# Casting and turning x three slices sooner, ahead of the next load in the SyncE queue

## The chip, the cores and the metric

The kernel runs on one core of one Trainium2 chip. The metric is device time in microseconds, as the median of several executions. Every execution also reports its span on the core and the mean granted clock of TensorE. An execution is called slow here when it is over 1.5% above the fastest of the same kernel; comparisons use the fast ones.

## The reference

For each of 8 batches (8 heads, 512 tokens, 32 state rows, head size 64), tokens and state attend to each other, and all rows then go through a gated layer:

```python
scores  = scale * x @ state.T          # 512 x 32 per head; softmax; xread = a  @ state
scores2 = scale * state @ x.T          # 32 x 512 per head; softmax; sread = a2 @ x
h   = concat([xread, sread])           # 544 rows per batch, 512 wide, for 8 batches
out = (relu(h @ w_gate) * (h @ w_val)) @ w_out      # 512 -> 1536 -> 512
```

## The kernel before

All matmuls are in bf16. The first two batches and the start of the third are written out as a list of first steps. A repeated part then runs one period per batch `s`, in 12 slices `jf`. In period `s` TensorE computes the gated layer of batch `s`. In the gaps the kernel computes the scores of batch `s+1` and prepares x of batch `s+2`: x is cast to bf16 (`x_conv`), turned by a transposing DMA (`x_bar`) into the layout that the scores need, and copied beside columns of ones (`x_copy`) for the sread matmuls.

```python
def x_conv(b, h0, n, eng):      # b >= 2: xb (bf16) <- xf (fp32), half of the heads at a time
    ...
def x_bar(b):                   # "the turn": 16 blocks of 128 x 128, 512 KB in all
    nc.sync.dma_start_transpose(out=xT[b].rearrange("p c j t -> p (c j) t"), in_=xb[b])
def x_dma(b, ...):              # "the load": 1 MB of x into xf (two buffers)
    ...  nc.sync.dma_start(out=xf[b][:, lo:lo + n], in_=x_rows(b, lo, n))
...
def nxt(n, jf):                 # n = s + 2
    if n >= B:
        return
    if jf == 6:
        xb_alloc(n)
        at_alloc(n)
        x_conv(n, 0, 4, "p")    # "p": GpSimd
    elif jf == 7:
        x_conv(n, 4, 4, "p")
        if n + 1 < B:
            x_dma(n + 1)
    elif jf == 9:
        x_bar(n)
    elif jf in (10, 11):
        x_copy(n, 2 * (jf - 10), 2, "p")

for s in range(2, B):
    for jf in range(NF):
        gv(s, jf)
        if jf in (3, 9):
            continue
        outp()                  # a third of an output tile; each third one evicts and issues a store
        for k in ((jf - 1, jf) if jf in (4, 10) else (jf,)):
            aux(s + 1, k)       # jf 0, 1: scores; 2, 3: normalise; 4: turn of the weights (ans)
            nxt(s + 2, k)
        if jf in (2, 8):
            ...                 # projections of w by the state (u_mm), their evictions, sread at 8
```

Loads, turns and stores all go through the SyncE queue, which in the traces issues them in program order and waits at each for what that one needs: in before an output stood in the queue from 69.6 us until its eviction let it go at 73.41, and the turn behind it went out at 75.06. From 60 to 192 us the outputs waited 18 times for their evictions, 71.5 us in all.

The softmax here doesn't subtract the row's maximum and nothing guards it: scores larger than these inputs give would overflow.

Of the kernel before, what the change touches and what calls it, by code (L numbers as in the profile page):

```python
# [67 lines left out]
def kernel(  # L68
# [55 lines left out]
    def cp(eng, o, i):  # L124
        if eng == "a":
            nc.scalar.copy(out=o, in_=i)  # L126
        elif eng == "v":
            nc.vector.tensor_copy(out=o, in_=i)  # L128
        else:
            nc.gpsimd.tensor_copy(out=o, in_=i)  # L130
# [22 lines left out]
    def x_dma(b, lo=0, n=H, after=None):  # L153
        if b not in xf:
            xf[b] = xin.tile([128, H, NC, D], FP32, name="xf", tag="xf")
        d = nc.sync.dma_start(out=xf[b][:, lo:lo + n], in_=x_rows(b, lo, n))  # L156
        loads["x", b, lo] = d.ins.name
        gate(d, after)
# [48 lines left out]
    def xb_alloc(b):  # L207
        xb[b] = att.tile([128, NC * H * D], BF16, name="xb", tag="xb", bufs=2)

    def at_alloc(b):  # L210
        xT[b] = att.tile([128, NC, NJ, 128], BF16, name="xT", tag="xT")
        e_sn[b] = att.tile([128, NC, 2, NJ, Ns], BF16, name="e_sn", tag="e_sn")
        asn[b] = att.tile([128, NC, 2, NJ, Ns], BF16, name="a_sn", tag="a_sn")
        cs[b] = small.tile([128, NC, 2, NJ], FP32, name="cs", tag="cs")
        rc[b] = small.tile([128, NC, 2, NJ], FP32, name="rc", tag="rc")
        ANS[b] = anspool.tile([128, NC, 2, 128], BF16, name="ans", tag="ans")
# [8 lines left out]
    def xs_rows(b, h0, n):  # L225
        v = xs(b)[:, :, h0 // 2:(h0 + n) // 2, 2:130]
        return v.rearrange("p c j (s d) -> p j s c d", s=2)

    def x_conv(b, h0, n, eng):
        src = xf[b][:, h0:h0 + n]  # L230
        if b < 2:
            cp(eng, xs_rows(b, h0, n), src.rearrange("p (j s) c d -> p j s c d", s=2))
        else:
            cp(eng, xb[b].rearrange("p (c h d) -> p h c d", h=H, c=NC)[:, h0:h0 + n], src)

    def x_copy(b, c0, n, eng):
        cp(eng, xs(b)[:, c0:c0 + n, :, 2:130],
           xb[b].rearrange("p (c j m) -> p c j m", c=NC, j=NJ)[:, c0:c0 + n])
# [12 lines left out]
    def x_bar(b):  # L251
        nc.sync.dma_start_transpose(out=xT[b].rearrange("p c j t -> p (c j) t"), in_=xb[b])
# [257 lines left out]
    def nxt(n, jf):  # L510
        if n >= B:
            return
        if jf == 6:
            xb_alloc(n)
            at_alloc(n)
            x_conv(n, 0, 4, "p")
        elif jf == 7:
            x_conv(n, 4, 4, "p")
            if n + 1 < B:
                x_dma(n + 1)  # L520
        elif jf == 9:
            x_bar(n)
        elif jf in (10, 11):
            x_copy(n, 2 * (jf - 10), 2, "p")

# [6 lines that stand above are left out]
            outp()  # L532
            for k in ((jf - 1, jf) if jf in (4, 10) else (jf,)):
                aux(s + 1, k)
                nxt(s + 2, k)
            if jf in (2, 8):
                if s + 1 < B:
                    if jf == 2:
                        u_alloc(s + 1)
                    else:  # L540
                        sr_mm(s + 1)
                    u_mm(s + 1, 768 * (jf // 8), 768)
                    if jf == 8:
                        sr_ev(s + 1)
                    for i, e in enumerate("avavav"):
                        u_ev(s + 1, 768 * (jf // 8), 768, i, e)
                outp()
# [36 lines left out]
```

## Time and profile before

| | before |
|---|---|
| time, three runs that the prediction knew | 225.16 us (224.95 to 225.21) |
| span of the profiled run | 222.4 us |
| TensorE busy | 215.7 us, 97% |
| VectorE, ScalarE, GpSimd busy | 63%, 51%, 19% |
| one period of the repeated part | 23.3 us |

In the profile PE is TensorE's matmuls, PEld its weight loads, DVE VectorE, ACT ScalarE, POOL GpSimd, SPq the SyncE queue. `xT<-xb` is the turn of x, `xf<-in_x_dram` the load of x, `sc_ps` the scores, which are the first readers of the turned x.

### The profile page before, as it was taken

How to read it: one execution, taken by the hardware profiler on the slowest of the kernel's cores; microseconds unless marked ns; L12 is line 12 of the kernel's file. 1: busy time of each engine (PE TensorE's matmuls, PEld its weight loads, DVE VectorE, ACT ScalarE, POOL GpSimd, SP SyncE). 2: the span in 40 equal slices, each digit the busy share in tenths (PEclk: the TensorE clock that was granted, in tenths of full speed). 3: DMA queues.
4: the chain of work that ended last, by engine and by line, in shares of the span. 5: the costliest groups of instructions: out<-in, count | busy, mean ns of one | idle time of the engine just before them, and what ended most of it. 6: DMA issues, size and time to landing. Idle time of an engine off the chain costs nothing.

```text
span 222.4 us, 4870 instructions
## 1 busy us (share of the span) xinstructions
PE 215.7 (97%) x1953; PEld 105.2 (47%) x1953; DVE 141.1 (63%) x245; ACT 114.4 (51%) x212; POOL 41.8 (19%) x51
## 2 busy tenths in 40 slices
PE   6979999999999999999999999999999999999994
PEld 3544434444444444444444444444444444586543
DVE  5789798697395748764786659565956543452210
ACT  3768776655463647364636374545546343343111
POOL 6498005064070330016000700000000000000000
PEclk9999999999999999999999999999999999999999
DMA  6999998979936831576138811351131111111133
GB/s 187 246 225 200 220 246 149 236 215 144 283 104 146 249 86 47 107 234 142 48 73 264 134 48 36 101 123 50 47 94 58 47 47 50 47 47 41 57 77 112
DMA packets 43575, 28.17 MB, mean 127 GB/s; under 512 B 23840, under 2 KB 39328, under 8 KB 43552
## 3 DMA queue, kind: packets, MB, share of 16 engines
q1 hardware_dynamic: 36688, 23.14, 39.3%
q0 software_dynamic: 6864, 4.72, 14.2%
q8 instruction: 15, 0.25, 0.4%
q14 instruction: 8, 0.07, 0.1%
HBM read 18.35 MB, written 8.91 MB: 123 GB/s over the span
## 4 chain that ended last, share of the span: by engine, by line
PE 89%; DMA 7%; DVE 1%; SPq 1%; issue 0%; ACT 0%
PE o_ps L414 38%; PE gv_ps L377 37%; PE u_ps L325 6%; PE gvs_ps L399 5%; DMA xf<-in_x_dram 4%; DMA xT<-xb 2%; PE sc_ps L260 1%; PE o_ps L439 1%; PE sr_ps L306 1%; SPq L156 1%; PE aT_ps L288 1%; DVE xs L128 1%; DVE U L128 0%; DVE ans L128 0%; SPq L142 0%
## 5 line engine op out<-in xcount | busy, mean ns | idle before, releaser
L386 DVE TENSOR_TENSOR h_sb<-gv_ps,g_sb 128x512 bf16<-128x512 f32 x96 | 65.5, 688 | 49.2 <-ACT g_sb L383 48.9
L377 PE MATMUL gv_ps<-ans,U 128*128 128x512 bf16 x384 | 94.5, 379 | 0.0
L414 PE MATMUL o_ps<-wo_sb,h_sb 128*128 128x512 bf16 x372 | 94.1, 379 | 0.0
L383 ACT ACTIVATE g_sb<-gv_ps 128x512 bf16<-128x512 f32 x96 | 57.3, 597 | 54.5 <-PE gv_ps L377 53.9
L377 PEld LDWEIGHTS <-U 128*128 128x128 bf16 x384 | 36.0, 98 | 42.1 <-issue 1.4
L414 PEld LDWEIGHTS <-h_sb 128*128 128x128 bf16 x372 | 35.3, 98 | 43.3 <-issue 4.0
L126 ACT CAST U<-u_ps 128x512 bf16<-128x512 f32 x52 | 27.7, 595 | 5.8 <-PE u_ps L325 5.2
L128 DVE CAST U<-u_ps 128x512 bf16<-128x512 f32 x44 | 27.7, 674 | 0.8 <-PE u_ps L325 0.8
L130 POOL CAST xb<-xf 128x1024 bf16<-128x1024 f32 x11 | 11.2, 1040 | 71.3 <-DMA xf<-in_x_dram 71.3
L126 ACT COPY o_sb<-o_ps 128x512 f32<-128x512 f32 (+2 forms) x20 | 10.8, 540 | 18.7 <-PE o_ps L414 17.1
L128 DVE COPY o_sb<-o_ps 128x512 f32<-128x512 f32 (+2 forms) x18 | 11.5, 637 | 9.1 <-ACT o_sb L126 4.5
L271 ACT ACTIVATE e_sn<-sc_ps 128x512 bf16<-128x512 f32 (+1 forms) x18 | 9.8, 552 | 9.8 <-PE sc_ps L260 9.8
L130 POOL COPY xs<-xb 128x1024 bf16<-128x1024 bf16 x11 | 11.2, 1042 | 1.0 <-DVE xb L128 0.7
L403 DVE TENSOR_TENSOR hs_sb<-gvs_ps,g_sb 128x256 bf16<-128x256 f32 x12 | 5.1, 425 | 9.8 <-ACT g_sb L402 9.8
L277 DVE TENSOR_REDUCE cs<-e_sn 128x32 f32<-128x1024 bf16 (+2 forms) x13 | 10.4, 801 | 0.4 <-ACT e_sn L271 0.2
L325 PE MATMUL u_ps<-wg_sb,stT 64*32 64x256 bf16 (+1 forms) x280 | 10.2, 315 | 0.0
L325 PEld LDWEIGHTS <-stT 64*32 64x32 bf16 x560 | 6.0, 90 | 8.5 <-issue 6.9
L402 ACT ACTIVATE g_sb<-gvs_ps 128x256 bf16<-128x256 f32 x12 | 4.6, 384 | 10.2 <-PE gvs_ps L399 7.8
L325 PE MATMUL u_ps<-wv_sb,stT 64*32 64x256 bf16 (+1 forms) x280 | 9.7, 309 | 0.0
L468 PE MATMUL warm_ps<-warm 128*128 128x256 bf16 x37 | 7.0, 314 | 1.1 <-DVE warm L470 1.1
L260 PEld LDWEIGHTS <-xT 128*128 128x128 bf16 x128 | 5.9, 98 | 4.3 <-DMA xT<-xb 0.9
L260 PE MATMUL sc_ps<-stT,xT 128*128 128x64 bf16 x128 | 7.0, 193 | 0.5 <-ACT xT L126 0.3
(52 smaller groups left out, 110.2 us busy)
## 6 DMA issues: line engine op xcount, KB each, us to landing
out_dram<-o_sb SPq DMA_DIRECT2D x31, 256.0 KB, 2.4
xf<-in_x_dram SPq DMA_DIRECT2D x6, 1024.0 KB, 6.9
xf<-in_x_dram SPq DMA_DIRECT2D x8, 256.0 KB, 4.6
wo_sb<-in_moe_w_out_dram POOLq DMA_DIRECT2D x3, 512.0 KB, 16.1
wg_sb<-in_moe_w_gate_dram POOLq DMA_DIRECT2D x4, 256.0 KB, 6.3
wv_sb<-in_moe_w_val_dram POOLq DMA_DIRECT2D x4, 256.0 KB, 7.0
wg_sb<-in_moe_w_gate_dram POOLq DMA_DIRECT2D x1, 512.0 KB, 9.4
wv_sb<-in_moe_w_val_dram POOLq DMA_DIRECT2D x1, 512.0 KB, 12.0
```

The lines of the kernel that those rows point to most:

```text
L126: nc.scalar.copy(out=o, in_=i)
L128: nc.vector.tensor_copy(out=o, in_=i)
L130: nc.gpsimd.tensor_copy(out=o, in_=i)
L260: nc.tensor.matmul(ps_sc[b, kc][:, c, :, j2], xT[b][:, c, j], stT[:, b, j].rearrange("p (s n) -> p s n", s=2), start=True, stop=True)
L271: nc.scalar.activation(out=esl(e_sn, b, kc, j2, n).rearrange("p k j n -> p k (j n)"), in_=ps_sc[b, kc].rearrange("p c s j n -> p (c s) j n ...
L277: nc.vector.reduce_sum(out=c, in_=e, axis=AX.X)
L325: nc.tensor.matmul(ps[32 * j:32 * j + 32, 0:n], stT[r, b, j, 32 * kc:32 * kc + 32], wsb[w][r, j, lo:lo + n], start=(i == 0), stop=True, sk ...
L377: nc.tensor.matmul(ps.rearrange("p (c t) -> p c t", c=NC), U[b][:, kc, w, f0:f0 + 128], ANS[b][:, :, kc], start=(kc == 0), stop=(kc == 1))
L383: nc.scalar.activation(out=g_sbs[b, jf], in_=ps_g[b, jf][0], func=AF.Relu)
L386: nc.vector.tensor_tensor(out=hsb[b][:, jf], in0=ps_g[b, jf][1], in1=g_sbs[b, jf], op=ALU.mult)
L399: nc.tensor.matmul(ps[:, w].rearrange("p (b n) -> p b n", b=B), wsb[w][:, j, f0:f0 + 128], brT[:, :, 32 * j:32 * j + 32], start=(j == 0), ...
L414: nc.tensor.matmul(o_ps[0], src[:, jf, t0:t0 + 128], wo_sb[:, jf], start=(jf == 0), stop=(jf == NF - 1))
```

## The change

The intent is to give the turn of x more room before the scores need it: the casts are emitted at slices 3 and 4 instead of 6 and 7, and the turn at slice 6, where it now stands ahead of the load of the next x.

```diff
-        if jf == 6:
+        if jf == 3:
             xb_alloc(n)
+            x_conv(n, 0, 4, "p")
+        elif jf == 4:
+            x_conv(n, 4, 4, "p")
+        elif jf == 6:
             at_alloc(n)
-            x_conv(n, 0, 4, "p")
+            x_bar(n)
         elif jf == 7:
-            x_conv(n, 4, 4, "p")
             if n + 1 < B:
                 x_dma(n + 1)
-        elif jf == 9:
-            x_bar(n)
         elif jf in (10, 11):
```

## The prediction

Passages are cut from the text, with the cuts marked. Where the text says "this order" it means a load issued behind a turn; such a load landed after 7.1 us, 0.2 us over the median of 6.9. "No loss" means that VectorE was not slower beside GpSimd. The trace of before also shows in what sense TensorE is pipelined: a 512-column matmul is recorded with 0.38 us, and one starts every 0.216. "TensorE's own rate" stands for these 216 ns at clock 1.00 without a wait and for nothing more.

> **What bounds the kernel now.** I read the page's parts 1 and 4 first, then the busy table by stretches of one period, then the waits of TensorE inside the loop, then the SyncE timeline around one turn of x.
>
> ```profile
> PE 215.7 (97%) x1953; PEld 105.2 (47%) x1953; DVE 141.1 (63%) x245; ACT 114.4 (51%) x212; POOL 41.8 (19%) x51
> PE 89%; DMA 7%; DVE 1%; SPq 1%; issue 0%; ACT 0%
> PE o_ps L414 38%; PE gv_ps L377 37%; PE u_ps L325 6%; PE gvs_ps L399 5%; DMA xf<-in_x_dram 4%; DMA xT<-xb 2%; PE sc_ps L260 1%; PE o_ps L439 1%; PE sr_ps L306 1%; SPq L156 1%; PE aT_ps L288 1%; DVE xs L128 1%; DVE U L128 0%; DVE ans L128 0%; SPq L142 0%
> ```
>
> TensorE matmuls are 89% of the chain that ended last. The tempting item is "DMA xT<-xb 2%", the very transfer that the change moves; the question is which of the six turns it is. The table of busy time over one prologue-to-loop stretch and four periods of the loop says where TensorE still stands idle (columns: stretch, length, then busy time and count of PE, PEld, DVE, ACT, POOL, clock, DMA share, GB/s):
>
> ```profile
> 52.00:75.00 23.00, 22.84 (x236) 10.37 (x235) 15.36 (x27) 11.68 (x21) 5.28 (x6) 1.00 0.80 193
> 75.00:98.30 23.30, 23.30 (x210) 10.74 (x209) 15.88 (x26) 12.34 (x23) 4.05 (x4) 1.00 0.47 122
> 98.30:121.60 23.30, 23.30 (x210) 10.73 (x209) 15.90 (x26) 12.34 (x23) 4.05 (x4) 1.00 0.47 127
> 121.60:144.90 23.30, 23.30 (x210) 10.70 (x209) 15.88 (x26) 12.34 (x23) 4.05 (x4) 1.00 0.39 89
> 144.90:168.20 23.30, 23.30 (x210) 10.71 (x209) 15.88 (x26) 12.34 (x23) 0.00 (x0) 1.00 0.31 81
> ```
>
> TensorE is busy for 23.30 of 23.30 us in each of four periods. The only idle time near the loop is 0.16 us in the first row. It belongs to the x turn issued at 51.89 and landing at 57.4, which is the last one written out in the list of first steps, not in the repeated part. So the 2% of the chain is one turn of 5.5 us, and even that one made TensorE wait only 0.15 us (the timeline has 57.43 "sc_ps" with 0.15 of idle before it). The list of waits, restricted to 60 to 192 us, is empty for TensorE's matmuls; for its weight loads it holds only small issue gaps of at most 0.4 us, none of them on a DMA. The rest of the 6.7 us that TensorE is idle lies in the first 16 us (16.00 less 12.58 busy = 3.4) and after the last matmul (about 2.8), where the change does nothing.
>
> Busy alone could flatter a pipelined engine, so I checked the rate: four 512-column matmuls start every 0.86 us (79.02, 79.89, 80.75 in the timeline), 216 ns each, at clock 1.00 and in every period alike. The loop runs at TensorE's own rate.
>
> The SyncE queue in the loop's second period, and the turn's readers:
>
> ```profile
> 67.28 1.25 SPq L294 DMA_TRANSPOSE ans<-a_sn  x1
> 68.62 0.53 SPq L424 DMA_DIRECT2D out_dram<-o_sb  x1
> 69.20 0.43 SPq L156 DMA_DIRECT2D xf<-in_x_dram  x1
> 73.41 0.33 SPq L424 DMA_DIRECT2D out_dram<-o_sb  x1
> 73.84 1.12 SPq L317 DMA_TRANSPOSE brT<-srn  x1
> 75.06 2.03 SPq L252 DMA_TRANSPOSE xT<-xb  x1
> ```
>
> The load of x goes out at 69.20, the turn at 75.06, after an output that waits for its eviction and after the small brT turn. The turn lands 4.3 us after issue, at 79.4; its first weight load is at 80.5. So it is hidden, with 1.1 us to spare.
>
> [...] The trace has exactly this order once, at 51.89 and 53.98: the turn landed at 57.4, the load 7.1 us after its issue, at 61.1, against a median of 6.9. [...] The trace shows no loss: GpSimd is busy from 61.16 to 65.28 and idle from 84 to 93, and VectorE's 1024-element reduction takes 1.21 us in both (61.56 and 84.87), three U evictions 1.82 in both.
>
> **The change part by part.** No instruction is added or removed: the same 8 casts of 1.04 us, 8 copies of 1.04 us, 4 turns and 3 loads in the repeated part, n = 4 to 7.
>
> *Cast emitted at slices 3 and 4 instead of 6 and 7.* GpSimd has nothing but casts and copies of x in the loop, and their order among themselves is unchanged. It runs ahead of the others: what ended its idle time before the casts is always the landing of x (57.0 us over four waits from 60 us on), never its place in the program. The casts of n = 4 start at 61.16, of n = 5 at 75.55, of n = 6 at 99.40, of n = 7 at 122.55, each right as its x lands, and the last three a whole period before the turn that reads them. Earlier emission moves none. 0 us.
>
> *Turn at slice 6, ahead of the load.* Its input for n = 4 is ready at 61.16 + 2 x 1.04 = 63.2; the queue reaches the new place after the output, at 68.62 + 0.53 = 69.15. So it issues at about 69.2, 5.9 us sooner than 75.06. Landing takes 4.3 to 5.5 us (an ans turn issued at 67.28 is still on its way, as in the 5.5 us case), so at 73.5 to 74.7, and the slack to 80.5 grows from 1.1 to about 6 us. Slack now, the other periods: issue 99.16 + 4.3 = 103.5 against 103.8 (0.3); 121.72 + 5.3 = 127.0 against 127.16 (0.2); 145.00 + 4.3 = 149.3 against 150.5 (1.2). Each is thin but positive; all four grow by about 6. Time taken off TensorE's path in this trace: 4 x 0 = 0.
>
> *The load behind the turn.* It waits for the turn's 2.03 us of issue: from 69.20 to about 71.3. With the 7.1 us of the same order seen before, x lands at about 78.4 instead of 75.5, some 3 us later (up to 5 if it queues for the whole turn). Casts and copies shift by as much: casts at 78.4 to 80.5, copies to 82.5. The next reader of the cast is the turn at slice 6 of the next period, 92.6: about 12 us of slack. The copy's reader, the sread matmuls, is a period later still (119.3). The load of n = 7, cast at 122.55 now, comes at about 126; its turn moves to about 138.6 and still finds it ready. 0 us.
>
> *The outputs behind.* The next output in the queue waits until 73.41 for its eviction; the queue is free by about 72.9 (71.3 plus at most the 1.55 us that the load's issue took at 53.98). Even a delay of 2 us is covered by four output buffers filled every 23.3 / 4 = 5.8 us. 0 us.
>
> Sum: 0 us on the path, 225.16 stays. I shade it to **225.0 us** for the thin slacks below.
>
> **The rivals.** *A hidden wait that the profile just missed.* Slacks of 0.2 and 0.3 us are smaller than the scatter of a turn (landing from 4.3 to 5.5 us). The profiled run took 224.15 us, while the timed ones took 225.16; perhaps in those the turns come late. If each of the four landed 1 us later than here, TensorE would wait 0 + 0.7 + 0.8 + 0 = 1.5 us at most, less what later buffers absorb; the change would bring that back: 223.7 to 224.7. For it: the slacks. Against it: the trace has not one such wait, and the 1 us can as well lie at the start. One in six.
>
> *The load of x becomes the late one.* It shifts 3 to 5 us; the slack is 12. It would need the load to take three times 6.9 us. Against it: DMA share in the loop is 0.39 to 0.47. It would make 225 to 227. Under one in thirty.
>
> *GpSimd's copies collide with VectorE at the U evictions*, since they shift by 3 us. Six PSUM tiles fill at once there, and a slow VectorE would hold TensorE. Against it: the stretch from 61 to 65 us has exactly this overlap, without a gap on TensorE and with unchanged VectorE times. If it came, about 0.2 us a period, 225.8.
>
> *The gain of 2% that part 4 seems to promise* (5.5 us, 219.6) would need a TensorE wait in the loop to take away; there is none.
>
> **Range and chances.** The three runs before spread over 0.26 us. The first rival stretches the range down by up to 0.8, the third up by 0.6: 224.2 to 225.6. A move of 2% is 4.5 us, which exceeds all TensorE idle time that any transfer could be blamed for in the loop, so within 2% has 0.98.
>
> **What would show it.** Right: turns issued right after the output at slice 6 (near 69, 92, 115 and 138), landed 5 us or more ahead of their weight loads; x loads issued 2 us later and landing 3 us later, GpSimd's casts with them; TensorE busy 23.30 of 23.30 in each period; no waits for TensorE from 60 to 192. Wrong: a TensorE wait on the sc_ps group or in the period after a load; a period other than 23.3; a span over 223.5 or under 221.5, or timed runs 1 us lower with the profile's span unmoved, which would mean that the runs without a profile had the hidden wait.

## The result and the profile after

The changed kernel took 224.94 us (median of six runs, 224.56 to 225.32). The kernel before took 224.75 us over six runs (224.14 to 225.21). The ratio is 1.0009, with a 95% interval from 0.9987 to 1.0031: no change. Ratios here and below come from the fast runs of both kernels in the same rounds, so they are not quite the ratio of the medians quoted.

The busy table of the changed kernel, for the same five stretches that the prediction shows of before (stretch, length, busy time and count of PE, PEld, DVE, ACT, POOL, clock, DMA share, GB/s):

```profile
52.00:75.00 23.00, 22.96 (x237) 10.42 (x236) 15.47 (x27) 11.56 (x22) 5.86 (x6) 1.00 0.79 173
75.00:98.30 23.30, 23.30 (x210) 10.73 (x209) 15.88 (x26) 12.34 (x24) 4.05 (x4) 1.00 0.46 126
98.30:121.60 23.30, 23.30 (x210) 10.73 (x209) 15.90 (x26) 12.34 (x24) 4.05 (x4) 1.00 0.48 125
121.60:144.90 23.30, 23.30 (x210) 10.71 (x209) 15.88 (x26) 12.34 (x24) 4.05 (x4) 1.00 0.49 123
144.90:168.20 23.30, 23.30 (x210) 10.72 (x209) 15.87 (x26) 12.34 (x24) 0.00 (x0) 1.00 0.19 58
```

TensorE is again busy for the whole of each period, and VectorE and ScalarE do the same work in the same time. Only the DMA columns changed: in the fourth row the share rose from 0.39 to 0.49, in the last it fell from 0.31 to 0.19, because the last turn now lies before 144.9. The list of TensorE matmul waits from 60 to 192 us is empty, as before.

The SyncE queue in the loop's first period after the change, with the queue's lines in order of time (start, length of issue):

```profile
67.74 1.25 SPq L294 DMA_TRANSPOSE ans<-a_sn  x1
69.09 0.53 SPq L424 DMA_DIRECT2D out_dram<-o_sb  x1
69.72 2.23 SPq L252 DMA_TRANSPOSE xT<-xb  x1
72.00 0.85 SPq L156 DMA_DIRECT2D xf<-in_x_dram  x1
73.88 0.33 SPq L424 DMA_DIRECT2D out_dram<-o_sb  x1
74.30 1.43 SPq L317 DMA_TRANSPOSE brT<-srn  x1
```

The turn went out right behind the output, at 69.72 instead of 75.06. The load moved from 69.20 to 72.00. The output behind it still waits for its own eviction: 73.88 against 73.41, which is the 0.47 us by which everything in this run is later. That offset is there before the repeated part begins (the turn from the list of first steps was issued at 52.47 here and at 51.89 in before), so it is not an effect of the change.

The lines of the tile xT for this turn and its readers, before (the window ends after the first eight readers):

```profile
L260 PEld LDWEIGHTS <-xT x8: 98/98/98, 80.5 to 80.9; 128*128 128x128 bf16 x8
L252 SPq DMA_TRANSPOSE xT<-xb x1: 2027/2027/2027, 75.1 to 75.1; - x1
DMA to landing us min/median/max: 4.3/4.3/4.3
```

and after the change:

```profile
L260 PEld LDWEIGHTS <-xT x16: 98/98/98, 81.0 to 83.3; 128*128 128x128 bf16 x16
L252 SPq DMA_TRANSPOSE xT<-xb x1: 2225/2225/2225, 69.7 to 69.7; - x1
DMA to landing us min/median/max: 4.5/4.5/4.5
```

The turn lands at 69.7 + 4.5 = 74.2, and the first weight load that reads it is at 81.0. The slack is 6.8 us instead of 1.1. In the later periods it is 6.8, 6.3 and 6.3 us. All of it is unused.

GpSimd's casts of x for batches 5 and 6, before:

```profile
75.55 2.03 POOL L130 CAST xb<-xf 128x1024 bf16<-128x1024 f32 x2 [10.28 <-DMA xf<-in_x_dram]
99.40 2.03 POOL L130 CAST xb<-xf 128x1024 bf16<-128x1024 f32 x2 [19.74 <-DMA xf<-in_x_dram]
```

and after:

```profile
79.60 2.03 POOL L130 CAST xb<-xf 128x1024 bf16<-128x1024 f32 x2 [13.92 <-DMA xf<-in_x_dram]
101.97 2.03 POOL L130 CAST xb<-xf 128x1024 bf16<-128x1024 f32 x2 [18.26 <-DMA xf<-in_x_dram]
```

The brackets hold GpSimd's idle time and what ended it. Although the casts are emitted three slices sooner, they run later, since GpSimd had always been waiting for the load and the load is now behind the turn.

One line of the page did change in a way that could mislead. The chain that ended last, after:

```profile
PE 89%; DMA 5%; DVE 1%; ACT 1%; SPq 1%; POOL 1%; issue 0%; POOLq 0%
PE o_ps L414 38%; PE gv_ps L377 37%; PE u_ps L325 5%; PE gvs_ps L399 5%; DMA wv_sb<-in_moe_w_val_dram 3%; DMA xf<-in_x_dram 2%; PE sc_ps L260 1%; PE o_ps L439 1%; PE sr_ps L306 1%; SPq L156 1%; DVE h_sb L386 1%; ACT g_sb L383 0%; DVE cs L277 0%; POOL wg_sb L162 0%; POOL a_sn L283 0%
```

"DMA xT<-xb 2%" is gone from the chain, and yet nothing was gained. It was the turn in the list of first steps, which the change does not touch; in this run the chain happens to run through other steps of the start.

### The profile page after: what moved, and what is told of

It is laid out like the page before. It is cut to its first block, busy times and chain, and to the rows that moved or that the text cites. A ratio compares the mean times of both kernels' runs of the same rounds, so it can differ in the third digit from the quotient of the medians.

```text
span 222.8 us, 4872 instructions
## 1 busy us (share of the span) xinstructions
PE 216.4 (97%) x1953; PEld 105.5 (47%) x1953; DVE 141.1 (63%) x245; ACT 114.4 (51%) x212; POOL 42.0 (19%) x51
## 4 chain that ended last, share of the span: by engine, by line
PE 89%; DMA 5%; DVE 1%; ACT 1%; SPq 1%; POOL 1%; issue 0%; POOLq 0%
PE o_ps L414 38%; PE gv_ps L377 37%; PE u_ps L325 5%; PE gvs_ps L399 5%; DMA wv_sb<-in_moe_w_val_dram 3%; DMA xf<-in_x_dram 2%; PE sc_ps L260 1%; PE o_ps L439 1%; PE sr_ps L306 1%; SPq L156 1%; DVE h_sb L386 1%; ACT g_sb L383 0%; DVE cs L277 0%; POOL wg_sb L162 0%; POOL a_sn L283 0%
```

## The experiments

Theory A is the prediction's: TensorE sets the time, all turns were hidden with 0.2 to 1.2 us of slack, and the change only adds slack. It can be tested where it makes a strong claim: a turn that is only a little later must cost time at the old place and none at the new one. The rivals are that the place does not matter in either direction (B), that the casts matter (C), that timed runs without a profile had hidden waits (D), that the delayed load costs what the turn gains (E), and that GpSimd collides with VectorE (F). All ten kernels gave correct results.

**e1_turn_late: the turn later instead of sooner.**

```diff
 # on the kernel before
-        elif jf == 9:
-            x_bar(n)
         elif jf in (10, 11):
             x_copy(n, 2 * (jf - 10), 2, "p")
+            if jf == 11:
+                x_bar(n)
```

> The kernel before, with the turn of x emitted two steps later (slice 11), so that it stands behind one more output in the SyncE queue. Theory A (TensorE sets the time, each turn was hidden with 0.2 to 1.2 us of slack, so moving it earlier buys nothing and moving it later past the slack costs directly): the output is issued at 79.94 in the trace of before, so the turn is issued at about 80.3 and lands 4.3 to 5.5 us later, at 84.6 to 85.8, against a first weight load at 80.5. TensorE waits 4.1 to 5.3 us in each of four periods: 16 to 21 us more, 241 to 246 us. Rival B (the place of the turn does not matter, because the scores have slack behind them too, or something else absorbs it): under 2% more.

Measured: 248.53 us against 225.24 for before in the same rounds. The two fast runs, 245.87 and 246.28, give a ratio of 1.091 (1.082 to 1.101); two slow runs took 250.77 and 251.00, at a lower clock (0.959 and 0.952 against 0.979). The queue and the first late scores:

```profile
81.67 0.33 SPq L424 DMA_DIRECT2D out_dram<-o_sb  x1
82.11 2.18 SPq L252 DMA_TRANSPOSE xT<-xb  x1
```

```profile
86.60 0.56 PE L260 MATMUL sc_ps<-stT,xT 128*128 128x64 bf16 x8 [3.96 <-DMA xT<-xb]
```

The turn is held behind an output that waits for its eviction, and TensorE waits 3.96 us; the other three periods have 3.99, 3.94 and 3.88. That is what theory A said of the waits (16 at least, 15.8 found), and B falls. The time rose by more than the waits, though. The busy table around the first wait and over the loop shows why:

```profile
82.00:86.00 4.00, 0.64 (x3) 0.10 (x1) 0.69 (x1) 0.00 (x0) 0.00 (x0) 1.00 0.91 197
86.00:90.00 4.00, 3.40 (x16) 1.47 (x17) 0.69 (x1) 1.19 (x2) 0.00 (x0) 0.59 0.02 4
60.00:215.00 155.00, 139.24 (x1097) 62.25 (x1096) 85.70 (x134) 67.75 (x120) 16.19 (x16) 0.93 0.33 89
```

After the wait, TensorE's granted clock falls to 0.59 for the next 4 us, and over the loop it averages 0.93. A late turn is paid twice. (This profile is of a slow run; the fast ones lost less clock, as the figures above show. Their times are at the upper end of the expected 241 to 246 us, because the expectation counted the waits alone.)

**e2_casts_only: one part of the change alone.**

```diff
 # on the kernel before: casts at 3 and 4, the turn stays at 9
-        if jf == 6:
+        if jf == 3:
             xb_alloc(n)
+            x_conv(n, 0, 4, "p")
+        elif jf == 4:
+            x_conv(n, 4, 4, "p")
+        elif jf == 6:
             at_alloc(n)
-            x_conv(n, 0, 4, "p")
         elif jf == 7:
-            x_conv(n, 4, 4, "p")
```

> One part of the change alone: the casts at slices 3 and 4, the turn where it was before. Theory A: GpSimd runs ahead and its casts start when x lands, so every cast starts where it did in before (61.2, 75.6, 99.4, 122.6, within the 0.5 us by which starts of runs differ), ratio 1.000 within 0.3%. Rival C (the earlier place in the program lets GpSimd start sooner, and the turn's move spoils that gain in the changed kernel): casts start earlier than in before and the time falls by 0.3% or more.

Measured: 224.45 us, ratio 0.9965 (0.9902 to 1.0027), span 222.3 against 222.4. The casts start at 75.67, 99.61 and 122.55, against 75.55, 99.40 and 122.55: within 0.2 us. Emitting them sooner moves nothing, so C falls by its starts; the 0.3% in the mean is inside the interval.

**e3_double_old and e4_double_new: the same lateness at the old place and at the new one.** The turn is issued twice, with the same data and destination.

```diff
 # e3, on the kernel before               # e4, on the changed kernel
         elif jf == 9:                    #         elif jf == 6:
             x_bar(n)                     #             at_alloc(n)
+            x_bar(n)                     #             x_bar(n)
                                          # +           x_bar(n)
```

> The kernel before with the turn of x issued twice in a row at its old place (same data, same destination; the scores wait for the second). Theory A: the second turn lands at least one issue time, 2.0 us, and at most a whole turn, 4.3 us, later. Less the slacks of 1.1, 0.3, 0.2 and 1.2 us, TensorE waits 0.8 + 1.7 + 1.8 + 0.8 = 5.1 us at least and 14.4 us at most: 230 to 239 us. Rival B: within 1%.

> The changed kernel with the turn of x issued twice in a row at its new place. Theory A: the slack there is about 6.5 us (landing 74.2 against a first weight load at 81.0), so a second turn of 2.0 to 4.3 us is hidden and the time stays at 224.5 to 225.5; the load behind it lands another 2 to 4 us later and is hidden too. If Rival B holds, it is the same as well, but then e3 is the same too. If the delayed load is what matters, it is slower by 1% or more.

Measured: e3 248.22 us, ratio 1.100 (1.093 to 1.107); e4 225.12 us, ratio 0.9994 (0.9927 to 1.0061). The queue of e3 and one of its late scores:

```profile
77.21 6.19 SPq L252 DMA_TRANSPOSE xT<-xb  x2
```

```profile
173.02 0.60 PE L260 MATMUL sc_ps<-stT,xT 128*128 128x64 bf16 x8 [2.84 <-DMA xT<-xb]
```

The second turn starts 4.3 us after the first, when that has landed, so the whole 4.3 us counts. The four waits are 2.79, 3.95, 5.13 and 2.84, together 14.7 us, just above the expected 5.1 to 14.4. The mean clock was 0.965, and 246.6 us of span times 0.035 is, by estimate, another 8.6 us: together 23.3 of the 24.2 us by which the span grew. The expectation left the clock out, and so its 230 to 239 us were missed by 9. In e4 the loop has neither a wait nor a lower clock:

```profile
60.00:192.00 132.00, 132.00 (x1107) 60.50 (x1104) 86.53 (x136) 67.81 (x120) 16.22 (x16) 1.00 0.49 121
```

So the change does what it was made for. It buys slack that absorbs a whole second turn, which costs 10% at the old place. The unmodified kernel never draws on it.

**e5_after_again: are there hidden waits without a profile?** The changed kernel, unaltered, in five rounds.

> The changed kernel unaltered, timed in five rounds against before. Theory A: ratio 1.000, within 0.2%. Rival D (in executions without a profile the turns of before came late by a little, and the change brings back up to 1.5 us): ratio 0.993 to 0.998, with an interval that excludes 1.

Measured: 225.13 us against 225.50, ratio 0.9982 (0.9949 to 1.0015). The interval holds 1 and rules out a gain of 1.5 us (0.67%); the first comparison, with a lower end of 0.9987, leaves at most 0.3 us. D is not supported; a hidden wait of a few tenths of a us stays possible. Part of the scatter is the clock's: among the fast runs of both kernels, those with a mean clock of 0.990 to 0.992 took 225.89 to 226.70 us. Without them the means are 224.84 (five runs of the changed kernel) and 225.05 (seven of before).

**e6_load_late: the load of the next x later still.**

```diff
 # on the changed kernel
-        elif jf == 7:
-            if n + 1 < B:
-                x_dma(n + 1)
         elif jf in (10, 11):
             x_copy(n, 2 * (jf - 10), 2, "p")
+            if jf == 11 and n + 1 < B:
+                x_dma(n + 1)
```

> The changed kernel with the load of the next x put off from slice 7 to slice 11, where it stands behind one more output in the SyncE queue. Theory A: the load is issued at about 80.9 instead of 72.0 and lands at about 88, casts end at 90 and the turn that reads them is issued at about 93.1: about 3 us of slack left, so 224.5 to 225.5. Rival E (the load's landing is what the kernel is sensitive to, so that the change's delay of it eats a gain of the earlier turn): slower by 0.5% or more.

Measured: three fast runs at 223.96, 225.23 and 225.86 (one slow at 227.93), ratio 1.0041 (0.9985 to 1.0097), and the profiled span was 222.2 us. The load was issued at 80.1 instead of 72.0 and the casts ran at 86.96; TensorE has no wait in the loop. E falls: another 8 us of delay is hidden too. The run also showed a collision that the changed kernel avoids, where the copies end at 83.72 and the product starts at 89.84. VectorE's product for the softmax weights, before:

```profile
89.38 1.22 DVE L283 TENSOR_TENSOR a_sn<-e_sn,rc 128x1024 bf16<-128x1024 bf16 x1
```

and in e6, where GpSimd's copies of x fall on it:

```profile
89.20 1.97 DVE L283 TENSOR_TENSOR a_sn<-e_sn,rc 128x1024 bf16<-128x1024 bf16 x1
```

```profile
89.05 3.02 POOL L130 COPY xs<-xb 128x1024 bf16<-128x1024 bf16 x2
```

The product takes 1.97 instead of 1.22 us and the two copies 3.02 instead of 2.03. The product has two inputs in SBUF. The sum, which has one, and the evictions, which read PSUM, kept their 1.21 and 0.6 us beside GpSimd's copies in e7. What the product and the copies collide in was not shown. The collision costs the kernel nothing: the turn of these weights goes out at 91.23 and lands 3.1 us later, and the first matmuls that read it start at 102.15.

**e7_copies_x3: twice the GpSimd work.**

```diff
 # on the changed kernel
         elif jf in (10, 11):
-            x_copy(n, 2 * (jf - 10), 2, "p")
+            for _ in range(3):
+                x_copy(n, 2 * (jf - 10), 2, "p")
```

> The changed kernel with each GpSimd copy of x done three times, so that GpSimd is busy 8 us of each period instead of 4 and its copies run into the sum, the U evictions and the product on VectorE. Theory A: VectorE's instructions keep their durations (1.21 us for the 1024-element sum, 0.6 us for an eviction) or TensorE's buffers hide it; 224.5 to 225.5. Rival F (GpSimd's shift collides with VectorE and costs TensorE): slower by 0.3% or more, with longer VectorE instructions beside GpSimd.

Measured: 224.51 us, ratio 0.9966 (0.9927 to 1.0005). GpSimd is busy for 33.9 instead of 16.2 us between 60 and 192 us, VectorE for 86.5 in both, TensorE for 132.0 of 132.0. F falls as a cost to the kernel. VectorE's product kept its mean of 1.21 us. In one period the copies did reach it, and then GpSimd bore the delay. The product and the copy beside it:

```profile
66.50 1.22 DVE L283 TENSOR_TENSOR a_sn<-e_sn,rc 128x1024 bf16<-128x1024 bf16 x1
```

```profile
L130 POOL COPY xs<-xb x1: 2043/2043/2043, 66.6 to 66.6; 128x1024 bf16<-128x1024 bf16 x1
```

This copy takes 2.04 us instead of 1.04. In e6 a copy had started first (89.05 against 89.20), and there the product was slowed.

**e8_load_first: the order in the queue alone undone.**

```diff
 # on the changed kernel
         elif jf == 6:
             at_alloc(n)
-            x_bar(n)
         elif jf == 7:
             if n + 1 < B:
                 x_dma(n + 1)
+            x_bar(n)
```

> The changed kernel with the turn at slice 7 and behind the load of the next x, instead of at slice 6 ahead of it: the order of the queue alone is undone, the turn stays early. Theory A: the load is issued at 69.7 and lands at about 76, as in before; the turn is issued at about 70.2 and lands by 77 even if it stands behind the whole load, still 4 us ahead of the scores. 224.5 to 225.5. If the order ahead of the load matters, it differs from the changed kernel by 0.3% or more.

Measured: 225.56 us, ratio 1.0006 (0.9965 to 1.0046). The queue in the first period:

```profile
70.63 0.43 SPq L156 DMA_DIRECT2D xf<-in_x_dram  x1
71.17 5.77 SPq L252 DMA_TRANSPOSE xT<-xb  x1
```

Behind the load, SyncE needs 5.77 us to issue the turn instead of 2.23, and the turn lands 7.7 us after the start of its issue instead of 4.5. That is still three us early (78.9 against 81.9; four were expected). In the next period much less is left:

```profile
94.51 6.33 SPq L252 DMA_TRANSPOSE xT<-xb  x1
```

```profile
L260 PEld LDWEIGHTS <-xT x16: 98/98/98, 105.2 to 107.6; 128*128 128x128 bf16 x16
DMA to landing us min/median/max: 9.9/9.9/9.9
```

The turn lands at 104.4, 0.8 us ahead of its reader; in the third period (issued at 118.18, landing after 9.3 us, reader at 128.6) it is 1.1 us ahead, and in the fourth, which has no load, 6.2. With the changed kernel's order these slacks are 6.8, 6.3 and 6.3 us. So the order ahead of the load is worth 4 to 6 us of slack wherever there is a load, and the earlier slice behind the load would have left two turns within the 0.2 to 1.2 us of before. None of it is worth time to the kernel.

**e9_late_filled: is the surplus of e1 the clock's?** 34 idle matmuls ahead of the late scores keep TensorE active while it would wait.

```diff
 # on e1
         if jf == 0:
+            if n > 3:
+                fill(n, 34)        # 34 matmuls of zeros, 128 x 256, into the scores' own PSUM tile
             sc_mm(n, 0)
```

> The kernel of e1 (turn at slice 11) with 34 idle matmuls of 256 columns put ahead of the first scores of each of the four periods; they write into the scores' own PSUM tile, which the scores then overwrite, so the result stays right. At 107 ns each (half of the 216 ns of a 512-column matmul) they fill 3.6 us of the 3.9 us that TensorE waited in e1. Theory G (e1's 26.6 us of extra span are 15.8 us of waiting and some 10 us of matmuls at half clock after each wait): the filled wait keeps the granted clock at 1.00, the wait shrinks to about 0.3 us each, and the time is 225 + 16 = 240 to 242. Theory H (the excess over the wait is not the clock's but comes from other work delayed by the late scores): 245 to 249 as e1.

Measured: 244.89 us (fast runs 242.77, 244.74 and 245.05; one slow), ratio 1.084 (1.078 to 1.090). The loop of e9's profile, to be held against the last row of e1's table:

```profile
60.00:215.00 155.00, 150.16 (x1251) 75.93 (x1266) 88.33 (x138) 69.33 (x124) 16.19 (x16) 1.00 0.35 90
```

The clock stays at 1.00 where e1 had 0.93. The time fell by less than expected, and one has to take the loop alone to see why. From the first scores of the first to those of the fourth period, before takes 150.68 - 80.75 = 69.9 us, e1 175.86 - 86.60 = 89.3, e9 171.31 - 87.44 = 83.9. Of e1's surplus of 19.3 us, three waits are 11.8; the other 7.5, or 2.5 per period, is gone in e9 but for 0.7, so it was lost clock. Of e9's surplus of 13.9 us, three fillings (34 x 107 ns each, an estimate) are 10.9 and the waits behind them (1.87, 0.25, 0.16) 2.3; 0.7 is left. So G (the surplus is the clock's) holds for the loop and H (it is other work delayed by the late scores) falls, but the total missed its range of 240 to 242 by 3 us: in the first two periods the turn landed only 5.4 and 6.1 us after issue, and the profiled run also lost clock in its first 16 us (0.89).

**e10_half_turn: shorter waits.**

```diff
 # on the kernel before
         elif jf == 9:
             x_bar(n)
+            x_bar_half(n)          # the same for 8 of the 16 blocks
```

> The kernel before, turn at its old place, followed by a second turn of half of the same data (8 of 16 blocks). In e3 the second turn was issued when the first had landed, 4.3 us later; half a turn should land as fast as an ans turn of 8 blocks, 3.1 us. Less the slacks of 1.1, 0.3, 0.2 and 1.2 us, TensorE waits 2.0 + 2.8 + 2.9 + 1.9 = 9.6 us. Theory G with a clock that falls only after waits of about 3 us or more (2.79 us kept 1.00 in e3, 2.84 and longer did not): clock 0.98 to 1.00, time 233 to 238. If any wait halves the clock for some 7 us: 3.5 us more for each, 247 to 249.

Measured: 240.12 us, ratio 1.064 (1.059 to 1.069), clock 0.972 to 0.979. The waits are 1.70, 2.35, 3.90 and 1.73, together 9.7 where 9.6 were expected; that the sum agrees so well is luck, since single waits are off by up to 1.0 us (the third, behind a first turn that took 6.6 us to land). The time lies 2 us above the range. The second of them, and the clock in the stretches after the first and the second:

```profile
111.43 0.39 PE L263 MATMUL sc_ps<-stT,xT 128*128 128x64 bf16 x8 [2.35 <-DMA xT<-xb]
```

```profile
86.00:90.00 4.00, 3.95 (x48) 1.90 (x54) 1.57 (x3) 2.44 (x5) 0.00 (x0) 1.00 0.01 4
111.50:116.00 4.50, 4.50 (x28) 2.07 (x28) 0.69 (x1) 1.76 (x4) 0.00 (x0) 0.62 0.00 0
```

After 1.70 us the clock stays at 1.00, and after 2.35 us it is 0.62. In e3 a wait of 2.79 us cost no clock and one of 2.84 us did. So the limit of about 3 us that I had put into the expectation is wrong, and the length of a wait alone does not decide. The clock records of the traces show a pattern: in the loops of e1, e3 and e10 all changes of the clock lie, for each run, on one grid of 3.41 us (in e3 at 111.61, 118.44, 142.34, 149.16, 173.06 and 176.47). A window here is the stretch from one point of this grid to the next. Cut along it, e3's waits of 2.79 and of 2.84 us look like this:

```profile
80.89:84.31 3.42, 2.17 (x11) 0.78 (x8) 1.87 (x3) 0.60 (x1) 1.40 (x2) 1.00 0.53 102
84.31:87.72 3.41, 1.87 (x16) 1.03 (x17) 0.25 (x1) 1.08 (x2) 0.00 (x0) 1.00 0.50 135
169.64:173.06 3.42, 0.58 (x5) 0.09 (x3) 0.60 (x1) 0.00 (x0) 0.00 (x0) 1.00 1.00 230
173.06:176.47 3.41, 3.41 (x16) 1.49 (x17) 0.69 (x1) 1.19 (x2) 0.00 (x0) 0.50 0.03 5
```

The first columns are the stretch, its length and TensorE's busy time; the clock is the third number from the end. The edge of a window cut the wait of 2.79 us into 1.25 and 1.54 us of idle time; the wait of 2.84 us lay within one window, and the next window ran at a clock of 0.50.

All waits in the loops of these three runs and of e9 fit. The clock fell at the end of every window with 2.25 us of idle time or more (nine) and after no wait of 1.87 us or less (e9's longest; e10 has 1.70 and 1.73); where the limit lies between the two is not shown. It came back at the end of the first window with little idle time (0.42 us at most; 0.90 and more was too much), so each fall lasted one or two windows, which at a clock of 0.50 is by estimate 1.7 or 3.4 us lost. By its mean clock of 0.979 (again an estimate) a fast run of e1 had some three windows at half clock, where its slow profile has six.

## Why the prediction was right

*The bound.* Right. TensorE's period is 23.30 of 23.30 us in both kernels, and the one idle moment near the loop is outside of what the change touches.

*The casts.* Right, 0 us: e2 shows them alone. In the full change they came later by 3.6, 2.1 and 2.3 us (after taking off this run's offset of 0.46), where the prediction had some 3.

*The turn.* Right. (The lines that the prediction calls the loop's second period are of its first.) Issue was predicted at 69.2 and came at 69.72, landing 4.5 us later within 4.3 to 5.5. The slack of about 6 us came out as 6.3 to 6.8. The thin slacks of before were real: e3 and e10 turn them into waits whose sums (14.7 and 9.7 us) are what the slacks give when the added time is known (14.4 and 9.6). In the fourth period the turn went out at 139.65; the predicted 138.6 had left out the 0.53 us of issue of the output before it.

*The load behind the turn.* Right within 1 us. It was issued at 72.0 instead of 71.3, and landed 7.5 us later instead of 7.1. Its slack is real too: e6 spends 8 us more of it for nothing.

*The outputs behind.* Right: the queue was free at 72.85, and the next output went out at its own time.

*The rivals.* The hidden wait, for whose sake I shaded the number to 225.0, was not found: the two comparisons leave room for some tenths of a us at most. The medians lie 0.2 us above and 0.4 us below before in two sets of rounds, which is scatter. That 225.0 came within 0.1 us of the median measured is luck: single runs of the changed kernel range from 224.56 to 225.32, and before itself moved from 225.16 to 224.75 with three more runs. For the collision on GpSimd's side, the prediction looked at the wrong evidence: it cited the sum and the U evictions, which kept their 1.21 and 0.6 us beside the copies in e7, while the instruction that slowed down, to 1.97 us, is the product with two inputs in SBUF (e6). The conclusion held, because the turn that waits for that product lands some 8 us before its reader.

*What I had not seen.* The size of the cost when the slack runs out. I put a wait into e1, e3 and e10 at its own length; lost clock added a third to two thirds to that (by estimate 5.1 us, 0.021 of 244 us, in the fast runs of e1, whose profile has 15.8 of waits; 8.6 to the 14.7 of e3). Had the change made the turn later instead of sooner, the prediction would have been wrong by that.

## What to carry to other kernels

A transfer that already beats its reader gave no time here when it was issued sooner, however thin its margin (0.2 to 1.2 us); look for the reader's wait in the trace, and read the chain of waits for which instance of the transfer it names. The value of such a move is robustness: test it by making the transfer late on purpose, at the old place and at the new one. In an in-order queue, ask what a transfer stands behind: two slices later, behind a store that waits for its eviction, cost 9% here, and most of the slack that the change bought came from standing ahead of the load. Here 2.25 us or more of idle time on TensorE within one window of 3.41 us was paid again in clock, all nine times that it occurred (e1, e3, e10).

## What the runs showed beside the change

- Gaps of 2.35 us (e10) and 2.84 us (e3) on TensorE already brought the clock down, to 0.62 and 0.57 over the next 4 to 5 us, while 1.70, 1.73 and once 2.79 us did not. What told them apart was the idle time within one window: 2.25 us of 3.41 was enough, and no wait of 1.87 us or less was.
- A turn of 16 blocks (512 KB) took 4.3 us at best from issue to landing and one of 8 blocks 3.1 (e10), so by an estimate from these two 0.15 us per block and some 1.9 us fixed; the turn brT of one block took 2.2 us at best in before, where this gives 2.05. For a turn of 16 blocks the fixed part is by this estimate nearly half.
- Where the turn was issued right behind the load in the same queue, SyncE was held for 5.77 to 6.33 us instead of 1.73 to 2.42, and the turn landed after 7.7 to 9.9 us instead of 4.4 to 4.9 (three periods of e8 against the changed kernel). In the other order the load took 6.0 to 7.5 us instead of 6.3 to 6.7 (changed kernel against before, in the loop).
